# Planned arrival of eight heads' loads, filling of PE's gaps, and ten products of zeros, in the head of a fused attention and feed-forward kernel

## The chip, the cores and the metric

The kernel runs on one core of one Trainium2 chip. The metric is the device time of one execution in microseconds. The median of three runs of the kernel before is 440.37 us (439.73 to 440.39).

In what follows PE is the engine for matrix products, DVE the vector engine, ACT the scalar engine, POOL the engine whose queue issues the loads, SP the engine whose queue issues the stores and the transposing transfers. SBUF is the working memory, PSUM the memory into which PE writes, in eight banks.

## The reference

Attention with a squared ReLU in place of the softmax, then a gated feed-forward network over the tokens. All is given as float32.

```python
batch, n_heads, seq, head_dim = (8, 12, 448, 64)        # q, k, v
n_tokens, d_model, d_ff = (3584, 768, 1536)             # w_gate, w_val: 768x1536, w_out: 1536x768

scores = scale * np.matmul(q, k.transpose(0, 1, 3, 2))
attn = np.maximum(scores, 0.0) ** 2 / S
attn_out = np.matmul(attn, v)
x = np.ascontiguousarray(attn_out.transpose(0, 2, 1, 3)).reshape(B * S, H * D)

rms = np.sqrt(np.mean(x * x, axis=-1, keepdims=True) + 1e-06)
xn = x / rms * rms_g
g = xn @ w_gate
silu = g * (1.0 / (1.0 + np.exp(-g)))
val = xn @ w_val
return (silu * val @ w_out).astype(np.float32)
```

## The kernel before

**Tiling.** A batch is 448 tokens. Its twelve heads are worked on as six pairs (`j` from 0 to 5), since two heads of 64 fill the 128 partitions; two pairs (`j`, `j + 1`) form one group of value products. Scores are made transposed: keys on the partitions, queries along the row. The 448 keys are three blocks of 128 and a rest of 64; the rests of two pairs share one tile (`rest`). Batch 0 is done in two halves of 224 queries (`HS`, `scores_half`), so that the feed-forward part can begin on the first half; later batches are done whole.

**Stages of batch 0.** For each pair `transposes(b, j)` turns k and q on PE into a bank of PSUM: 14 small products read k from `wo_sb` (the space of the output weights serves k of batch 0, line 420) and 8 read q from `qb` (line 428). Then a copy moves the turned pair from PSUM to `qkT` (line 438 on DVE, or on ACT; the planner chooses). `scores_half` makes score products (line 502) and `rest` the rest (line 520) into double banks `psS`; `evict_rect` takes them out with a ReLU, on ACT (line 468) or DVE (line 466), and squares them on DVE (line 471). `attend` makes the value products (line 606), after which come the eviction to `xT` (lines 652 and 654), squares for the norm, their sums on PE (line 921), ln and exp on ACT (lines 729 and 733) and six scalings on DVE (line 738). The first gate and value products of the feed-forward part (line 873) read these. All that comes before them is called the head here.

**What sets the order.** No order is written out by hand. `Planner` keeps a model of each engine's free time. An `Op` has a cost for each engine that may do it, its dependences, and a rank; `Planner.run` always starts what can start earliest, and the order in which it starts the work is the order in which instructions are issued. So a figure in the model changes no duration on the chip, but can change the order of instructions on an engine, the engine of a copy or of a ReLU, and the bank that is used. In the model a load lands when `arrives(kb, rate)` says: all loads share one stream (`dma_free`), which moves `kb` kilobytes at `rate` kilobytes per microsecond.

**Loads.** All go through POOL's queue, in the order of the calls at the end: q and k of batch 0 in four parts (heads 0 and 1, 2 and 3, 4 to 7, 8 to 11), v in two parts, the gate and value weights in four quarters each, then batch 1 and the output weights. `load` plans the parts of q and k whose last head is 2 or 8 (that is heads 0 and 1, and heads 4 to 7) with 300 kilobytes per microsecond, the other parts with 340.

**Products of zeros.** `ones_bf` and `busy_bf` (ones and zeros) feed products of 128x224 whose result nobody reads. The planner calls `fill(t0, t1, late)` before each piece of PE work: `t0` is when PE becomes free in the model, `t1` when the next work starts. In the stretch called early (5.5 to 20 us of the model) it fills gaps from 0.15 us on, and as if they were 0.1 us longer, 0.5 us where the next work is a transpose (`late`); a product counts as 0.1 us there and the fill stops 0.15 us short of the lengthened end. Before 5.5 us a product counts as 0.19. The zeros go into one of the single banks `psP`, if one is free.

The order of the head that the planner writes for PE, in short: 22 products of zeros while the first loads are under way, pairs 0 and 1 transposed one after the other with zeros between, scores of these pairs with zeros between, pairs 2 and 3 transposed, three more score blocks, seven zeros, one score block, pairs 4 and 5 transposed, scores, seven zeros, the first value products.

## Time and profile before

| | |
|---|---|
| median of three runs | 440.37 us |
| the profiled execution | 441.04 us |
| its span, from the first to the last instruction | 439.3 us |
| PE busy | 432.9 us |
| ACT busy | 263.7 us |
| DVE busy | 256.2 us |
| granted clock of PE over the span | 1.000 |
| first gate product (line 873) starts | 27.52 us |
| a product of zeros in the first four microseconds | 0.185 us (22 weight loads in 4.07 us) |

A row of the timeline gives start, duration, engine, line, operation, output and input, and how often it comes in a row; a bracket at the end says how long the engine had been idle before it and what ended this. PE's instructions are pipelined, so a row of products lasts longer than the time after which the next row starts. Times within the head are from the start of the span.

### The profile page before, as it was taken

How to read it: one execution, taken by the hardware profiler on the slowest of the kernel's cores; microseconds unless marked ns; L12 is line 12 of the kernel's file. 1: busy time of each engine (PE TensorE's matmuls, PEld its weight loads, DVE VectorE, ACT ScalarE, POOL GpSimd, SP SyncE). 2: the span in 40 equal slices, each digit the busy share in tenths (PEclk: the TensorE clock that was granted, in tenths of full speed). 3: DMA queues.
4: the chain of work that ended last, by engine and by line, in shares of the span. 5: the costliest groups of instructions: out<-in, count | busy, mean ns of one | idle time of the engine just before them, and what ended most of it. 6: DMA issues, size and time to landing. Idle time of an engine off the chain costs nothing.

```text
span 439.3 us, 17167 instructions
## 1 busy us (share of the span) xinstructions
PE 432.9 (99%) x7861; PEld 351.4 (80%) x7861; DVE 256.2 (58%) x462; ACT 263.7 (60%) x390; POOL 47.1 (11%) x67
## 2 busy tenths in 40 slices
PE   8999999999999999999999999999999999999996
PEld 6668877677778677789988997689988997788865
DVE  2987588647955675486756556666755356432210
ACT  3783497539946765686758665586657656342222
POOL 8522400012012001200300012001000000000000
PEclk9999999999999999999999999999999999999999
DMA  8999995699669957896792899079001300020013
GB/s 98 193 204 202 201 206 77 111 194 117 75 79 172 163 81 92 108 155 114 102 120 66 131 151 123 8 137 171 4 3 37 106 7 3 1 85 27 3 37 109
DMA packets 82680, 44.75 MB, mean 102 GB/s; under 512 B 41904, under 2 KB 79152, under 8 KB 82608
## 3 DMA queue, kind: packets, MB, share of 16 engines
q0 software_dynamic: 43232, 24.38, 41.2%
q1 hardware_dynamic: 38992, 18.94, 22.0%
q8 instruction: 61, 1.00, 0.9%
q10 hardware_dynamic: 384, 0.34, 0.3%
q14 instruction: 11, 0.09, 0.1%
HBM read 48.76 MB, written 11.01 MB: 136 GB/s over the span
## 4 chain that ended last, share of the span: by engine, by line
PE 96%; DMA 1%; DVE 1%; issue 1%; POOL 0%; ACT 0%; POOLq 0%
PE psP L873 77%; PE psS L606 8%; PE psS L484 6%; PE psP L1152 1%; PE psS L520 1%; PE psP L428 1%; PE psS L502 1%; DMA wo_sb<-in_k_dram 1%; PE psP L420 0%; POOL qb L300 0%; PE psP L921 0%; DVE hT L958 0%; POOL wo_sb L284 0%; ACT xn L657 0%; DVE x L711 0%
## 5 line engine op out<-in xcount | busy, mean ns | idle before, releaser
L873 PE MATMUL psP<-xn,wg_sb 64*64 64x448 bf16 (+1 forms) x2304 | 235.0, 338 | 0.2 <-ACT sil L944 0.2
L873 PE MATMUL psP<-xn,wv_sb 64*64 64x448 bf16 (+1 forms) x2304 | 217.7, 338 | 0.1
L468 ACT ACTIVATE r<-psS 128x896 bf16<-128x896 f32 (+1 forms) x162 | 144.0, 925 | 55.7 <-PE psS L484 28.3
L873 PEld LDWEIGHTS <-wg_sb 64*64 64x64 bf16 (+1 forms) x2304 | 132.0, 105 | 17.8 <-issue 3.3
L873 PEld LDWEIGHTS <-wv_sb 64*64 64x64 bf16 (+1 forms) x2304 | 132.0, 105 | 16.1 <-issue 3.0
L873 PE MATMUL psP<-wo_sb,hT 64*128 64x384 bf16 (+2 forms) x1562 | 139.6, 321 | 0.0
L471 DVE TENSOR_TENSOR r<-r 128x896 bf16<-128x896 bf16 (+1 forms) x165 | 98.9, 617 | 60.3 <-ACT r L468 59.4
L873 PEld LDWEIGHTS <-hT 64*128 64x128 bf16 (+1 forms) x1562 | 100.1, 97 | 23.4 <-issue 3.2
L958 DVE TENSOR_TENSOR hT<-sil,psP 128x448 bf16<-128x448 bf16 (+1 forms) x108 | 61.1, 566 | 57.8 <-PE psP L873 44.1
L944 ACT ACTIVATE sil<-psP 128x448 bf16<-128x448 f32 (+1 forms) x108 | 54.9, 509 | 59.9 <-PE psP L873 55.1
L1018 ACT COPY ost<-psP 128x384 f32<-128x384 f32 (+1 forms) x55 | 25.9, 475 | 43.3 <-PE psP L873 42.8
L484 PE MATMUL psS<-qkT 64*64 64x448 bf16 (+1 forms) x420 | 48.1, 351 | 0.0
L606 PE MATMUL psS<-r,vb 64*64 64x448 bf16 (+1 forms) x716 | 44.2, 335 | 0.8 <-issue 0.6
L738 DVE SCALAR_TENSOR_TENSOR xn<-xT,g_sb,rstd 128x448 bf16<-128x448 bf16 (+1 forms) x54 | 30.2, 629 | 22.2 <-ACT rstd L733 22.1
L300 POOL DMA_DIRECT2D vb<-in_v_dram x20 | 14.3, 737 | 199.7 <-PE psP L873 132.7
L606 PEld LDWEIGHTS <-vb 64*64 64x64 bf16 x756 | 25.9, 106 | 9.5 <-issue 3.0
L654 ACT ACTIVATE xT<-psS 128x896 bf16<-128x896 f32 (+1 forms) x25 | 21.4, 857 | 10.2 <-PE psS L606 10.1
L484 PEld LDWEIGHTS <-qkT 64*64 64x64 bf16 (+1 forms) x420 | 22.2, 103 | 5.0 <-issue 0.7
L391 ACT ACT_TABLE_LOAD x16 | 20.5, 1283 | 1.0 <-PEq L1227 0.7
L669 DVE TENSOR_TENSOR x<-xT 128x896 f32<-128x896 bf16 x14 | 15.2, 1087 | 3.6 <-ACT xT L654 3.6
L671 DVE TENSOR_TENSOR acc<-acc,x 128x896 f32<-128x896 f32 x14 | 15.3, 1092 | 0.5
L300 POOL DMA_DIRECT2D qb<-in_q_dram x12 | 10.2, 854 | 42.5 <-DVE acc L671 14.0
(60 smaller groups left out, 158.3 us busy)
## 6 DMA issues: line engine op xcount, KB each, us to landing
vb<-in_v_dram POOLq DMA_DIRECT2D x12, 384.0 KB, 6.6
qb<-in_q_dram POOLq DMA_DIRECT2D x6, 672.0 KB, 8.3
out_dram<-ost SPq DMA_DIRECT2D x7, 336.0 KB, 3.0
wg_sb<-in_moe_w_gate_dram POOLq DMA_DIRECT2D x4, 576.0 KB, 15.5
wv_sb<-in_moe_w_val_dram POOLq DMA_DIRECT2D x4, 576.0 KB, 17.5
wo_sb<-in_moe_w_out_dram POOLq DMA_DIRECT2D x2, 1152.0 KB, 14.4
kb<-in_k_dram POOLq DMA_DIRECT2D x6, 384.0 KB, 8.9
out_dram<-ost SPq DMA_DIRECT2D x8, 288.0 KB, 2.8
```

The lines of the kernel that those rows point to most:

```text
L300: dma = nc.gpsimd.dma_start(out=stage(nm, b)[prt, h0:h1, : (u1 - u0) * D], in_=src.rearrange("h (p u) d -> p h (u d)", p=n)[:, :, u0 * D : ...
L391: nc.scalar.add_instruction(mybir.InstLoadActFuncSet(name=name, act_func_set_id=n, ins=[], outs=[]))
L468: nc.scalar.activation(out=op.view, in_=src, func=ACT.Relu)
L471: nc.vector.tensor_tensor(out=rl.view, in0=rl.view, in1=rl.view, op=ALU.mult)
L484: nc.tensor.matmul(out=ps[m0:m1, hh, :S], lhsT=qkT[b][prt, j, 0, c * P + m0 : c * P + m1], rhs=qkT[b][prt, j, 1, :], start=True, stop=True,)
L606: mm = nc.tensor.matmul(out=ps[hh * D : (hh + 1) * D, jj, :w], lhsT=vb[prt, 2 * (j + jj) + hh, u * D : (u + 1) * D], rhs=r[prt, hh, :], st ...
L654: nc.scalar.mul(out=to, in_=src, mul=inv_attn)
L738: nc.vector.scalar_tensor_tensor(out=xns[b][:, kt, lo : lo + w], in0=xTs[b][:, kt, lo : lo + w], scalar=g_sb[:, kt : kt + 1], in1=rstd[:, ...
L873: mm = nc.tensor.matmul(out=self.ps[m0:m1, : self.w], lhsT=self.lhsT(i)[prt, m0:m1], rhs=self.rhs(i)[prt], start=(half == 0 and i == 0), s ...
L944: nc.scalar.activation(out=s[:, :w], in_=g.ps[:, :w], func=ACT.Silu)
L958: nc.vector.tensor_tensor(out=hT[:, fb, o : o + w], in0=sil[b, fb, lo][1][:, :w], in1=g.ps[:, :w], op=ALU.mult,)
L1018: nc.scalar.copy(out=to, in_=g.ps[:, :w])
```

## The change

Three edits. `load` plans heads 4 to 7 of q and k of batch 0 with 340 instead of 300 kilobytes per microsecond; since all loads share one stream, every later load lands earlier in the model too. `fill` no longer lengthens gaps; in the early stretch it fills gaps from 0.2 us on, and stops 0.1 us short of their end. And `transposes` puts five products of zeros into its own bank ahead of pairs 2 and 4 of batch 0; the planned cost of these two, 0.52 us, stays.

```diff
             if e == "PE" and self.fill is not None:
-
-                self.fill(self.free["PE"], t, 0.4 if op != "step" and op.form == "t" else 0.0)
+                self.fill(self.free["PE"], t)
...
-            ops = [pool_dma(0.7, D * U * D * 4 * (h1 - h0) / 1e3, 300.0 if h1 in (2, 8) else 340.0, runs_of_seven, deps)]
+            ops = [pool_dma(0.7, D * U * D * 4 * (h1 - h0) / 1e3, 300.0 if h1 == 2 else 340.0, runs_of_seven, deps)]
...
-            ops.append(pool_dma(0.72, kb, (300.0 if h1 in (2, 8) else 340.0) if b == 0 else 400.0, whole, deps))
+            ops.append(pool_dma(0.72, kb, (300.0 if h1 == 2 else 340.0) if b == 0 else 400.0, whole, deps))
...
+    def busy(tile):
+        nc.tensor.matmul(out=tile[:, :HS], lhsT=ones_bf[:], rhs=busy_bf[:, :HS], start=True, stop=True)
+
     def transposes(b, j):
...
             op.flat = flat
+            if b == 0 and j in (2, 4):
+
+                for _ in range(5):
+                    busy(op.ps.tile)
             for u in range(U if b == 0 else 0):
...
-    def fill(t0, t1, late):
+    def fill(t0, t1):
 
         early = 5.5 < t0 < 20.0
-        if not fill_on[0] or t1 - t0 < (0.15 if early else 0.3):
+        if not fill_on[0] or t1 - t0 < (0.2 if early else 0.3):
             return
-        if early:
-            t1 += 0.1 + late
...
-        while t0 + (0.19 if t0 < 5.5 else 0.1) <= t1 - 0.15:
+        while t0 + (0.19 if t0 < 5.5 else 0.1) <= t1 - (0.1 if early else 0.15):
             t0 += 0.19 if t0 < 5.5 else 0.1
-            nc.tensor.matmul(out=s.tile[:, :HS], lhsT=ones_bf[:], rhs=busy_bf[:, :HS], start=True, stop=True)
+            busy(s.tile)
```

In the program that the planner then writes, POOL's instructions are those of before, in the same order. PE has 71 products of zeros instead of 81. Pair 2's copy is on ACT instead of DVE. The transposes of pairs 4 and 5 stand ahead of the score block that stood before them. Of the score tiles of pairs 2 and 3, the last wide ReLU goes from ACT to DVE and the narrow one of the rest from DVE to ACT. Behind the last attention blocks of the head the order of PE is the same in both.

## Prediction

> **What bounds the kernel now.** First the page's table of engines, then the table of busy time by stretch, which says where each engine is full.

> ```profile
> PE 432.9 (99%) x7861; PEld 351.4 (80%) x7861; DVE 256.2 (58%) x462; ACT 263.7 (60%) x390; POOL 47.1 (11%) x67
> ```

> ```profile
> 10.00:15.00 5.00, 5.00 (x100) 3.50 (x96) 4.36 (x9) 3.38 (x6) 3.19 (x4) 1.00 1.32 174
> 15.00:20.00 5.00, 4.81 (x98) 2.99 (x92) 4.58 (x10) 3.89 (x7) 3.38 (x5) 1.00 1.38 203
> 20.00:25.00 5.00, 4.78 (x90) 2.87 (x87) 4.98 (x11) 4.83 (x8) 1.00 (x2) 1.00 1.30 201
> 28.00:35.00 7.00, 7.00 (x137) 5.60 (x135) 5.64 (x14) 5.25 (x10) 1.63 (x3) 1.00 1.32 204
> ```

> The columns are the stretch, its length, busy time of PE, weight loads, DVE, ACT and POOL, then clock and DMA. From 28 us PE has no gap: a saved microsecond there must be PE work, and the change touches none. Everything it does lies before the first gate product of the feed-forward part (27.52 us). In that head PE looks full too, but part of its work is products of zeros; the engine that is full of real work from 15 to 25 us is DVE (4.58 and 4.98 of 5 us). So the question is when DVE's chain ends, not how many zeros are dropped.

> The timeline of the head gives the rest (start, duration, instruction, in brackets the idle time before it and what ended it):

> ```profile
> 6.22 1.13 PE L1152 MATMUL psP<-busy_bf,ones_bf 128*128 128x224 bf16 x10
> ...
> 7.58 0.41 PE L420 MATMUL psP<-ident,wo_sb 64*64 64x64 bf16 x14 [0.23 <-DMA wo_sb<-in_k_dram]
> ...
> 11.60 0.41 PE L420 MATMUL psP<-ident,wo_sb 64*64 64x64 bf16 x14
> ...
> 12.36 1.28 DVE L438 COPY qkT<-psP 128x896 bf16<-128x896 bf16 x2 [0.61 <-PE psP L428]
> ...
> 13.62 0.84 PE L1152 MATMUL psP<-busy_bf,ones_bf 128*128 128x224 bf16 x7
> ...
> 14.69 0.41 PE L420 MATMUL psP<-ident,wo_sb 64*64 64x64 bf16 x14
> ...
> 16.25 0.21 PE L428 MATMUL psP<-ident,qb 112*64 112x112 bf16 x1 [0.19 <-issue]
> ...
> 16.50 0.62 DVE L438 COPY qkT<-psP 128x896 bf16<-128x896 bf16 x1 [0.42 <-PE psP L428]
> ...
> 17.88 0.58 PE L606 MATMUL psS<-r,vb 64*64 64x224 bf16 x16
> 18.11 0.62 DVE L466 TENSOR_SCALAR r<-psS 128x448 bf16<-128x448 f32 x1
> ...
> 20.01 1.09 DVE L466 TENSOR_SCALAR r<-psS 128x896 bf16<-128x896 f32 x1
> ```

> The reader is to see that DVE waits for PE twice (0.61 and 0.42 us) and then runs without a hole from 16.50 to 24.98 us. Last, the landings of the two late loads of k, by issue:

> ```profile
> wo_sb<-in_k_dram POOLq DMA_DIRECT2D x1, 224.0 KB, 6.6
> ...
> wo_sb<-in_k_dram POOLq DMA_DIRECT2D x1, 224.0 KB, 7.7
> ```

> Issued at 4.96 and 6.26 us, they land at 11.56 and 13.96 us.

> **The change, part by part.** *Loads.* The figures are the planner's alone. POOL's list in the built program is the same, instruction for instruction, so no transfer moves; cost 0. What moves is the order that the planner writes for PE, ACT and DVE.

> *Zeros.* The built program has 71 products of zeros instead of 81. Steady ones start 0.0975 us apart (ten from 6.22 us), so 0.98 us of PE goes. Where each piece went from:
> - 10 to 6 ahead of pair 1 (pairs of heads are 0 to 5): PE idles 0.4 us longer, but heads 2 and 3 of k land at 7.52 (issue 3.32 plus 4.2), so 7.58 stays. If they landed early, up to 0.4 us would be gained there, and pair 1's copy with it.
> - 3 to 2, 5 to 4, 6 to 5 (before 9.1, 10.7, 11.6): the work behind them waits for a DVE copy (ends 8.97), an ACT eviction (ends 10.45) and the landing at 11.56. These hide the saving; 0 each.
> - 7 to 5 ahead of pair 4, and 7 to 6 ahead of the first value products: below.

> *Pair 2's copy goes from DVE to ACT.* ACT sits idle from 11.69 to 13.31. No row shows this copy on ACT; it lies between 0.62 (DVE's copy of the same tile) and 0.92 us (ACT's 128x896 eviction). I take 0.91, nearest in engine and size. It starts after pair 2's transposes (12.55) and ends at 13.2 to 13.5. Behind it wait ACT's next eviction (13.31 before, at most 0.2 later; its square on DVE has 0.26 us to spare) and the five zeros into the same bank, which have until 13.96. Price 0 to 0.1, I take 0.

> *Pairs 4 and 5 ahead of the score block that stood before them.* Before: seven zeros from 13.62, a score block at 14.39 that waits for an eviction, transposes at 14.69. Now: three score blocks to 13.62 as before, then five zeros (seven took 0.77, so 0.55) to 14.17; k has landed at 13.96; transposes at 14.17. From the first transpose of pair 2 to the copy of pair 3 it took 11.60 to 13.02, 1.42, so DVE's copy of pair 5 starts at 15.59 instead of 16.50: 0.91 earlier. Of this 0.39 comes from the hole marked "issue" at 16.25, in which PE waited for nothing shown: without it the copy would have begun at 14.69 + 1.42 = 16.11. The hole may reappear at another instruction, so this part is worth 0 to 0.39.

> *What DVE then has to do.* Its list from that copy to the wide ReLU at 20.01 was: copy, two squares, the narrow ReLU (18.11), two squares, xn's square: 3.51 us. The new list has the same, but a wide ReLU in place of the narrow one, which ACT gets. From rows: a wide one occupies DVE 1.00 (20.01 to 21.01), the narrow one 0.53 (18.11 to 18.64). So 3.51 + 0.47 = 3.98; 15.59 + 3.98 = 19.57 against 20.01: 0.44 earlier, 0.05 if the hole stays (0.44 less its 0.39).

> *First value products.* They wait for ACT's eviction of their bank: ACT works 0.8 apart on evictions, its next score block ends on PE near 15.9, so the eviction (0.92) ends at 16.9, v's second load (about 7.5 plus 9.1, 16.6) is in, and they start near 17.0, 0.9 earlier than 17.88. But what follows waits for squares from DVE, which come only 0.05 to 0.44 earlier. This is where most of the 0.9 goes: into idle PE or other waits. From 20 us on the lists of DVE are the same, and the first gate product follows through ln, exp and six scalings, unchanged: 27.1 to 27.5.

> *After it.* PE's order differs nowhere behind the head's last attention blocks. An earlier start could meet the weights: the last quarter of w_val lands at 42.33 (18.93 plus 23.4) and is first used at 43.98, spare 1.65, the smallest of the eight; 0.44 passes.

> **Sum.** -0.05 to -0.44 from DVE's chain, 0 to +0.1 for the copy; I take -0.2, near the middle, since one trace doesn't tell whether the hole stays. Profiled span 439.3, so 439.1; the profiled execution took 441.04, 1.7 us more than its span, and the median of the runs is 440.37, 0.67 below it. Carried to the median: 440.2.

> [...] In the rows, the first 22 zeros took 4.07 us, 0.185 each, the later ones 0.0975: PE starts at half rate and was fast from about 5.5 us. All later rows of the head are fast; the granted clock's column says 1.00 throughout and doesn't show this start. [...] No row of this trace shows a second slow spell.

> **Rivals.** *Slower: PE drops to half rate once more.* [...] In the kernel before, 5.5 to 9.7 us had 16 zeros, and stayed fast; now 11, and about 0.8 us idle instead of 0.4. For it: the drop did exist at the start. Against: PE still works three quarters of that stretch. Price: a spell as long as the first (4.2 us, 1.29 to 5.5) loses half, 2.1, less the waits that it fills (0.8 + 0.2 + 0.2): about 0.9 to 1.2, so 441.4.

> *Faster: the zeros were the bound.* The chain of waits over the first 35 us gives them the largest share:

> ```profile
> by line: PE psP L1152 16.5%; PE psS L606 16.1%; PE psP L873 15.1%; PE psS L502 13.5%; DMA wo_sb<-in_k_dram 12.0%; PE psP L428 5.1%; PE psP L420 5.0%; POOL qb L300 4.1%; issue 3.3%; PE psS L520 3.1%; POOL wo_sb L284 1.6%; ACT xn L657 1.6%; P
> ```

> If PE's list alone set the head, ten fewer give 0.98 and the value products' 0.9 would carry through: 439.4. Against: zeros stand where something else is waited for, and DVE is full.

> *It does nothing beyond the plan.* Transfers are the same; if the moved work meets the same DVE chain with the hole in place, 440.3. This ends with my forecast.

> **How the numbers follow.** Runs of this kernel spread from 439.73 to 440.39, so 0.2% (0.88 us) is about what can be told from no change. Forecast 0.50, the third rival 0.17, half rate 0.20, zeros as the bound 0.13. The forecast's own range is 439.6 to 440.7 (the runs' spread about it). Down to 439.4 it takes in the faster rival, up to 441.4 the middle of the slower one. A gain over 0.88 needs nearly all of the faster rival, so faster 0.11; slower 0.21; same 0.68.

> **What would show it.** Right: transposes of pair 4 near 14.15, pair 2's copy on ACT at 12.6, first value products near 17.0, DVE's wide ReLUs at 16.8 and 19.7, first gate product at 27.1 to 27.5, span 438.9 to 439.3. Wrong: zeros or score products in the head 0.185 apart (half rate); pair 4 well after 14.3 (a late load); DVE with holes between 16 and 25 us and a first gate product before 26.8 (zeros were the bound); or a new wait after 28 us.

## The result and the profile after

The changed kernel took 439.64 us, the median of 22 executions (438.77 to 440.38); the kernel before on the same chip took 440.35 us, also of 22 (439.48 to 441.47). The ratio is 0.9984, 95% interval 0.9976 to 0.9991: 0.7 us faster, by the interval 0.4 to 1.1. That is within the 0.2% named as hard to tell from no change, but more than three times the forecast's 0.2 us. On a second chip the same kernel stood at 440.01 us against 440.25, ratio 0.9995, interval 0.9987 to 1.0004, which is not clear of 1. A ratio, here and below, is estimated from all executions against those of the kernel before on the same chip; it is not the quotient of the two medians and can lie a little beside it. The profiled execution took 439.62 us, with a span of 437.8 us; the span of before's was 439.3.

First the page's table of engines and the busy time by stretch of the changed kernel, with the columns that were explained for the kernel before:

```profile
PE 431.1 (98%) x7851; PEld 350.3 (80%) x7851; DVE 256.0 (58%) x461; ACT 264.0 (60%) x391; POOL 47.1 (11%) x67
```

```profile
10.00:15.00 5.00, 4.33 (x96) 3.04 (x94) 3.82 (x8) 3.75 (x6) 3.03 (x4) 1.00 1.35 185
15.00:20.00 5.00, 5.00 (x98) 3.14 (x94) 4.97 (x10) 4.07 (x7) 3.54 (x5) 1.00 1.36 202
20.00:25.00 5.00, 4.75 (x86) 2.81 (x85) 4.84 (x10) 4.83 (x8) 1.39 (x2) 1.00 1.32 203
28.00:35.00 7.00, 7.00 (x141) 5.50 (x140) 5.26 (x14) 4.98 (x10) 1.31 (x2) 1.00 1.31 203
```

From 10 to 15 us PE now stands idle for 0.67 us. From 15 to 20 DVE is full (4.97 of 5 us, 4.58 before). The timeline of the head shows where each piece went:

```profile
7.41 0.41 PE L426 MATMUL psP<-ident,wo_sb 64*64 64x64 bf16 x14 [0.61 <-DMA wo_sb<-in_k_dram]
...
11.88 0.41 PE L426 MATMUL psP<-ident,wo_sb 64*64 64x64 bf16 x14 [0.67 <-DMA wo_sb<-in_k_dram]
...
12.64 0.91 ACT L446 COPY qkT<-psP 128x896 bf16<-128x896 bf16 x1 [1.20 <-PE psP L434]
...
13.90 0.65 PE L411 MATMUL psP<-busy_bf,ones_bf 128*128 128x224 bf16 x5
14.48 0.41 PE L426 MATMUL psP<-ident,wo_sb 64*64 64x64 bf16 x14
...
15.24 1.28 DVE L444 COPY qkT<-psP 128x896 bf16<-128x896 bf16 x2
...
16.97 1.08 DVE L472 TENSOR_SCALAR r<-psS 128x896 bf16<-128x896 f32 x1
17.16 0.58 PE L612 MATMUL psS<-r,vb 64*64 64x224 bf16 x16
...
19.88 1.08 DVE L472 TENSOR_SCALAR r<-psS 128x896 bf16<-128x896 f32 x1
```

Pair 2's transposes begin at 11.88, later than before (11.60): PE waited 0.67 us for k. All that follows stands closer together, and the first gate product comes at 27.24 instead of 27.52 us.

That is 0.28 us, and the spans differ by 1.4 (439.26 less 437.84 is 1.42). Laying the same products of both traces side by side, the changed kernel is 0.38 us ahead everywhere from 31 to 146 us, 1.2 us ahead from 147 us, and 1.43 us ahead from about 165 us to the end. At 147 us the timeline of the kernel before has a hole in the middle of sixteen value products:

```profile
146.24 0.38 PE L606 MATMUL psS<-r,vb 64*64 64x448 bf16 x3
147.18 0.94 PE L606 MATMUL psS<-r,vb 64*64 64x448 bf16 x13 [0.56 <-issue]
147.78 0.54 PE L520 MATMUL psS<-qkT 64*64 64x448 bf16 x4
```

The changed kernel has none there:

```profile
145.86 0.95 PE L612 MATMUL psS<-r,vb 64*64 64x448 bf16 x16
146.62 0.38 PE L526 MATMUL psS<-qkT 64*64 64x448 bf16 x4
```

From the first value product to the rest it is 1.54 us before and 0.76 after: 0.78 us, in a place that no edit touches. The bracket says that PE waited for nothing that the profile shows; v for these products had landed some 10 us earlier.

### The profile page after: what moved, and what is told of

The parts are those of the page before. It is cut to its first block, busy times and chain, and to the rows that moved or that the text cites. A ratio compares the mean times of both kernels' runs of the same rounds, so it can differ in the third digit from the quotient of the medians.

```text
span 437.8 us, 17149 instructions
## 1 busy us (share of the span) xinstructions
PE 431.1 (98%) x7851; PEld 350.3 (80%) x7851; DVE 256.0 (58%) x461; ACT 264.0 (60%) x391; POOL 47.1 (11%) x67
## 4 chain that ended last, share of the span: by engine, by line
PE 95%; DMA 2%; DVE 1%; POOL 1%; issue 0%; ACT 0%; POOLq 0%
PE psP L879 77%; PE psS L612 8%; PE psS L490 6%; DMA wo_sb<-in_k_dram 2%; PE psS L526 1%; PE psP L434 1%; PE psS L508 1%; PE psP L411 1%; POOL qb L299 0%; PE psP L426 0%; PE psP L927 0%; POOL wo_sb L283 0%; DVE hT L964 0%; ACT xn L663 0%; DVE x L717 0%
## 5 line engine op out<-in xcount | busy, mean ns | idle before, releaser
L879 PEld LDWEIGHTS <-hT 64*128 64x128 bf16 (+1 forms) x1562 | 100.1, 97 | 23.4 <-issue 3.2
L490 PE MATMUL psS<-qkT 64*64 64x448 bf16 (+1 forms) x420 | 47.2, 351 | 0.0
L299 POOL DMA_DIRECT2D vb<-in_v_dram x20 | 14.3, 736 | 194.9 <-PE psP L879 188.1
L675 DVE TENSOR_TENSOR x<-xT 128x896 f32<-128x896 bf16 x14 | 15.2, 1087 | 3.6 <-ACT xT L660 3.6
L677 DVE TENSOR_TENSOR acc<-acc,x 128x896 f32<-128x896 f32 x14 | 15.3, 1092 | 0.5
## 6 DMA issues: line engine op xcount, KB each, us to landing
wg_sb<-in_moe_w_gate_dram POOLq DMA_DIRECT2D x4, 576.0 KB, 15.4
```

What stands on the lines that cost most here:

```text
L299: dma = nc.gpsimd.dma_start(out=stage(nm, b)[prt, h0:h1, : (u1 - u0) * D], in_=src.rearrange("h (p u) d -> p h (u d)", p=n)[:, :, u0 * D : ...
L490: nc.tensor.matmul(out=ps[m0:m1, hh, :S], lhsT=qkT[b][prt, j, 0, c * P + m0 : c * P + m1], rhs=qkT[b][prt, j, 1, :], start=True, stop=True,)
L879: mm = nc.tensor.matmul(out=self.ps[m0:m1, : self.w], lhsT=self.lhsT(i)[prt, m0:m1], rhs=self.rhs(i)[prt], start=(half == 0 and i == 0), s ...
```

## The experiments

Two things had to be told apart: what the edits do in the head, and whether the hole belongs to the change. A third question came from the slower rival: do the ten products keep PE's clock up?

**Both kernels again.** The kernel before, unchanged, one execution:

> The kernel before, unchanged, profiled once more, to see which of its holes marked 'issue' on PE come back (0.19 us at 16.25, 0.56 us at 147.18). If holes belong to the execution: both are absent or elsewhere, and the first gate product starts at 27.2 to 27.5. If they belong to the program's place in memory: both come back within 0.3 us of the same instruction. Span 438.0 to 440.5 either way.

It took 441.21 us, span 439.4. The hole in the head at 16.25 is gone; the one at 147 is there again, at the same product:

```profile
147.04 0.94 PE L606 MATMUL psS<-r,vb 64*64 64x448 bf16 x13 [0.34 <-issue]
```

The changed kernel, unchanged:

> The changed kernel, unchanged, profiled and timed once more. Theory 1 (DVE's chain in the head plus chance holes later): first gate product at 27.2 to 27.5, the same instruction at 60 us within 0.2 us of the first profile, time 0.2 to 0.7 us below the kernel before. Rival (the program's layout makes the holes): no hole over 0.3 us behind 30 us in this one either, time 0.7 us below.

It took 440.01 us (11 executions), as told above; span of the profiled one 437.5, first gate product at 26.90, no hole. So the hole at 16.25 was chance, and the one at 147 had come in both profiles of the kernel before and in neither of the changed one.

**One part at a time.** Only the loads' figures (340 instead of 300, as in the diff), on the kernel before:

> The kernel before with the new load plan alone (340 for heads 4 to 7): pairs 4 and 5 are transposed ahead of the score block, pair 2's copy is on ACT, fill as before, no five products. Theory 1 (the moved transposes feed DVE's chain earlier): the whole gain of the head, first gate product 0.2 to 0.4 us earlier than in the kernel before, time 439.9 to 440.2 against 440.4. Rival (fewer zeros bring it): first gate product as before, no gain.

439.75 us (12), ratio 0.9994, interval 0.9969 to 1.002. This edit alone gives the changed order of work. The first gate product comes at 27.12, yet the profiled span is 439.4, since a hole has opened in the same block of value products, ten products further on:

```profile
145.75 0.92 PE L606 MATMUL psS<-r,vb 64*64 64x448 bf16 x13
148.05 0.38 PE L606 MATMUL psS<-r,vb 64*64 64x448 bf16 x3 [1.39 <-issue]
```

Only the new filling, on the kernel before:

```diff
-        if not fill_on[0] or t1 - t0 < (0.15 if early else 0.3):
+        if not fill_on[0] or t1 - t0 < (0.2 if early else 0.3):
...
-            t1 += 0.1 + late
+            pass
...
-        while t0 + (0.19 if t0 < 5.5 else 0.1) <= t1 - 0.15:
+        while t0 + (0.19 if t0 < 5.5 else 0.1) <= t1 - (0.1 if early else 0.15):
```

> The kernel before with the new fill rule alone: 68 products of zeros instead of 81, order of the real work as before. Theory 1: zeros stand where something else is waited for, so the first gate product stays within 0.1 us and the time within 0.2 us of the kernel before. Rival (zeros were the bound): 13 fewer at 0.0975 us, up to 1.2 us earlier.

439.91 us (11), ratio 1.0003, interval 0.9984 to 1.0021; first gate product 26.64. Against the second profile of the kernel before (27.48) that is 0.84 us earlier, but 0.65 of it stands already at pair 2, which began at 11.30 instead of 11.95; behind pair 2 it is 0.19. Only the ten products, on the kernel before:

```diff
+            if b == 0 and j in (2, 4):
+                for _ in range(5):
+                    nc.tensor.matmul(out=op.ps.tile[:, :HS], lhsT=ones_bf[:], rhs=busy_bf[:, :HS], start=True, stop=True)
```

> The kernel before with the two times five products of zeros alone, fill and load plan as before (91 products of zeros). They stand behind zeros that already reach to the transposes, so each five (0.49 us) pushes the transposes back. Theory 1: from pair 1's first transpose to pair 2's takes 4.0 plus 0.5 = 4.5 us, from pair 2's first transpose to the first gate product 15.5 plus up to 0.5 us, time 440.7 to 441.4. Rival (the five products help by themselves, by keeping PE at full rate): no slower than the kernel before.

440.80 us (11), ratio 1.0017, interval 1.0002 to 1.0032: slower, with the first gate product at 27.87. With the old filling in place the ten are extra work on the path: pair 2 begins 4.49 us behind pair 1, where the kernel before took 4.02 and 4.01 in its two profiles.

**Zeros taken out of the changed kernel.** Without the ten products (`j in ()` in place of `j in (2, 4)`):

> The changed kernel without the two times five products of zeros (61 left); new load plan and new fill rule stay. Theory 1: pair 4's transposes wait for k's landing instead of the zeros, at most 0.2 us earlier; from pair 2's first transpose to the first gate product 15.2 to 15.4 us, as in the changed kernel (15.36); time within 0.3 us of it. Rival (the products are needed to keep PE at full rate): products in the head 0.185 us apart in some stretch, first gate product 0.9 us or more later.

442.31 us (10), ratio 1.0054, interval 1.0034 to 1.0073: the changed kernel less its ten products is slower than the kernel before. The busy time by stretch of this kernel shows why; the granted clock is the third number from the right:

```profile
14.00:15.00 1.00, 0.74 (x22) 0.68 (x22) 1.00 (x3) 1.00 (x2) 0.91 (x2) 0.70 1.46 191
15.00:16.00 1.00, 1.00 (x28) 0.79 (x24) 0.95 (x2) 0.79 (x2) 0.86 (x2) 0.50 1.45 195
...
20.00:21.00 1.00, 1.00 (x20) 0.59 (x20) 0.00 (x0) 0.27 (x1) 0.00 (x0) 0.50 1.25 192
21.00:22.00 1.00, 1.00 (x11) 0.32 (x7) 0.69 (x2) 1.00 (x3) 0.00 (x0) 0.89 1.33 204
```

And its timeline, where twelve score products last 1.23 us to the start of the zeros, and six zeros 1.24 to the next row (18.72); in the changed kernel it is 0.68 and 0.69:

```profile
11.91 0.41 PE L426 MATMUL psP<-ident,wo_sb 64*64 64x64 bf16 x14 [1.25 <-DMA wo_sb<-in_k_dram]
...
16.25 1.30 PE L508 MATMUL psS<-qkT 64*128 64x224 bf16 x12
17.48 1.30 PE L411 MATMUL psP<-busy_bf,ones_bf 128*128 128x224 bf16 x6
...
29.66 0.36 PE L879 MATMUL psP<-xn,wg_sb 64*128 64x224 bf16 x2
```

The clock is halved from 14.40 us (0.70 in a stretch of 1 us is 0.60 us at half rate) to 21.22: 6.82 us. The first gate product comes at 29.66, 17.75 behind pair 2's first transpose, where the changed kernel needs 15.36: 2.4 us more. This profile is of the slowest of the ten executions (445.01 us): besides the clock it has three holes, and the part behind its first gate product is 2.9 us longer than in the changed kernel.

Without any zeros that the planner writes between 5.5 and 20 us, the ten included (31 of 71 are left):

```diff
-            if b == 0 and j in (2, 4):
+            if b == 0 and j in ():
...
-        if not fill_on[0] or t1 - t0 < (0.2 if early else 0.3):
+        if early or not fill_on[0] or t1 - t0 < (0.2 if early else 0.3):
```

> The changed kernel without any product of zeros between 5.5 and 20 us of the plan: the 22 at the start and those behind 20 us stay, 31 in all. Theory 1 (zeros only fill waits, DVE's chain sets the end): PE's idle time in the head grows by some 2.5 us, the first gate product stays within 0.2 us of the changed kernel's place behind pair 2's transposes (15.36 us). Rival half rate: score products 0.15 us apart instead of 0.075 in some stretch of the head, first gate product 0.9 to 1.7 us later, time 440.5 to 441.5. Rival zeros as the bound: first gate product 0.5 us or more earlier.

442.20 us (8), ratio 1.0048, interval 1.0031 to 1.0066. The clock falls earlier, at 9.76 us, and stays down to 26.82:

```profile
9.00:10.00 1.00, 0.59 (x8) 0.29 (x5) 0.58 (x2) 1.00 (x2) 0.61 (x1) 0.88 0.99 118
10.00:11.00 1.00, 0.40 (x4) 0.13 (x3) 1.00 (x3) 1.00 (x3) 0.09 (x1) 0.50 1.19 151
...
26.00:27.00 1.00, 1.00 (x15) 0.45 (x15) 0.63 (x2) 1.00 (x2) 0.00 (x0) 0.59 1.31 203
```

The clock is not all of it here. Three of the eight executions have a mean granted clock of 0.999 or 1.000 and still took 442.04 to 443.04 us, longer than three with 0.983 to 0.988 (441.03 to 441.55). What these three lost stays open.

**Which five.** The ten products were then split, on the changed kernel. The five ahead of pair 2 alone (`j in (2,)`):

> The changed kernel with the five products ahead of the second pair kept and those ahead of the fourth left out (66 products of zeros). Theory A: TensorE's clock falls where it has stood or only transposed too long, and the longest such stretch is the wait for k ahead of the second pair (0.17 to 1.25 us in the runs so far) with the transposes right behind it; then the five there are what is needed, the clock stays at 1.00 through 14 to 21 us, 14 transposes take 0.26 to 0.32 us, the first gate product comes about 15.4 us after the second pair's first transpose, and the time is 439.6 to 440.1 us. Theory B: the five ahead of the fourth pair, where three pairs are transposed close together and PE waits for k again, are the ones that are needed; then the clock falls to 0.5 to 0.6 from 14 us on as without the ten, and the time is 442 to 443 us.

440.09 us (12), ratio 1.0003, interval 0.9979 to 1.0027. The five ahead of pair 4 alone (`j in (4,)`):

> The changed kernel with the five products ahead of the fourth pair kept and those ahead of the second left out (66 products of zeros). Theory A: the clock falls to 0.5 to 0.6 in the stretch 11 to 17 us, as without the ten, and the time is 442 to 443 us. Theory B: the clock stays at 1.00 and the time is 439.6 to 440.1 us. If both this kernel and the one with the five ahead of the second pair stay at 1.00, either five are enough; if both fall, all ten are needed.

441.81 us (12), ratio 1.0028, interval 1.0002 to 1.0055. Neither profile shows the clock down, but the mean granted clock of each execution does: 5 of 12 executions with the five at pair 4 have 0.988 to 0.991, and 2 of 12 with the five at pair 2 have 0.992. Neither five alone is enough, and the third outcome named there, that all ten are needed, is nearest. That the place ahead of pair 2 matters more, as theory A has it, is likely from 2 against 5 of 12, not shown. The profile with the five at pair 4 has two other losses instead:

```profile
14.84 0.41 PE L426 MATMUL psP<-ident,wo_sb 64*64 64x64 bf16 x14 [0.72 <-DMA wo_sb<-in_k_dram]
...
148.69 0.38 PE L526 MATMUL psS<-qkT 64*64 64x448 bf16 x2 [1.19 <-issue]
```

The first is the late part of k: when it lands late, the new order of pairs 4 and 5 waits for it. The profile with the five at pair 2 met an early one and shows what the five at pair 4 cost then: pair 4 starts at 13.74, 2.32 behind pair 2 instead of 2.60, and the first gate product at 26.51, the earliest of all.

**Two of three parts.** Loads' figures and ten products, with the old filling (91 products of zeros):

> The kernel before with the loads planned by the 340s and the ten products, and the old filling of gaps (91 products of zeros). If the gain of the change is the order of the work alone, this has the order and time of the changed kernel: first gate product 15.3 to 15.4 us behind the second pair's first transpose, 439.6 to 440.1 us. If zeros ahead of the pairs cost what the old filling and the ten put there, it is 0.3 to 0.5 us later, near the kernel before or above it (the ten alone on the kernel before gave 440.80 us).

439.92 us (12), ratio 0.9995, interval 0.9979 to 1.001; first gate product 27.08, 15.65 behind pair 2's first transpose. New filling and ten products, with the old figures (78 products of zeros):

> The changed kernel with the loads planned by the 300s as before (78 products of zeros): the new filling and the ten products on the old order of the work. If the new order is what gains, this has the time of the kernel before, 440.2 to 440.5 us; if the shorter filling gains and the ten products keep the clock up, 439.6 to 440.1 us and the first gate product 15.3 to 15.5 us behind the second pair's first transpose.

440.12 us (12), ratio 1.0, interval 0.9984 to 1.0016; first gate product 27.25, 15.93 behind. From pair 2's first transpose to the first gate product the two kernels with the new order and all ten products need 15.36 (changed) and 15.65, the two with the old order 15.93 and 16.11 (ten products only). Without the ten it is 15.53 before, 15.30 with the figures alone and 15.34 with the filling alone. So in these profiles, one or two of each kernel, either part shortens the head by 0.2 us, and it is the new order that makes room for the ten. But in the new order pair 4 stands one score block earlier in PE's list and can meet k still on its way: where it waited for k, by 0.72 us with the five at pair 4 and by 0.64 in the kernel shifted by 20 (below), the same stretch took 16.15 and 16.07, longer than in the kernel before. The medians of the last two kernels, 0.2 us apart with intervals of 0.16%, don't tell them apart.

**The hole.** If the place of an instruction in PE's list alone opened it, the changed kernel with 20 PE instructions more at its start would have its value products at the place of the kernel before. Four of the first 22 zeros are cut into fourteen small ones:

```diff
+            zeros[0] += 1
+            if zeros[0] <= 4:
+                for _ in range(4 if zeros[0] <= 2 else 3):
+                    nc.tensor.matmul(out=s.tile[:32, :D], lhsT=ones_bf[:, :32], rhs=busy_bf[:, :D], start=True, stop=True)
+            else:
+                busy(s.tile)
```

> The changed kernel with four of the 22 products of zeros at the start cut into 14 of 64 columns, same streamed columns. It adds 20 instructions on PE, so every later instruction has the place in the list that it has in the kernel before. Theory 1 (holes marked 'issue' belong to the execution): no difference, span 437.4 to 438.6, time within 0.3 us of the changed kernel. Rival (the place in the list decides): the hole of the kernel before at 147 us is back, three value products into their block, 0.3 to 0.9 us, and the time is 0.3 to 0.7 us above the changed kernel's.

440.09 us (12), ratio 1.0004, interval 0.9985 to 1.0023; no hole at 147 in its profile. The place alone does not open it. But it does say where a hole can be: counted from the start of PE's list, the holes near 147 us stand ahead of the same product, the 2524th, in every kernel that has one, whatever number of zeros comes before (the last section sets the starts of instruction packets beside them).

**All profiles, taken apart.** The work behind the first gate product is the same in all fourteen, 7446 products. Rest is the span less the first gate product's start; holes are the idle times of PE that the timeline marks "issue" behind it.

| kernel | zeros | first gate product | rest | holes (us, at) |
|---|---|---|---|---|
| before, again | 81 | 27.52, 27.48 | 411.8, 411.9 | 0.56 at 147; 0.34 at 147 |
| changed, again | 71 | 27.24, 26.90 | 410.6, 410.6 | none |
| figures only | 71 | 27.12 | 412.3 | 1.39 at 148 |
| filling only | 68 | 26.64 | 411.4 | 0.26 at 110 |
| ten products only | 91 | 27.87 | 410.7 | none |
| figures and ten | 91 | 27.08 | 410.9 | none marked |
| filling and ten | 78 | 27.25 | 411.3 | none marked |
| five at pair 2 | 66 | 26.51 | 410.7 | none |
| five at pair 4 | 66 | 27.60 | 412.3 | 1.19 at 149 |
| shifted by 20 | as changed, 4 cut | 27.30 | 411.0 | none |
| no ten products | 61 | 29.66 | 413.5 | 0.68, 1.16, 0.34 at 101, 152, 280 |
| no zeros 5.5 to 20 us | 31 | 30.69 | 411.3 | none marked |

A single product's row lasts 0.35 us there, while the next product starts long before its end (sixteen start within 0.76 us in the changed kernel), so a short stop leaves no idle time that could be marked. It shows in a row that lasts too long. With filling and ten products, the sixteen value products at 147 us take 0.52 us longer than in the changed kernel:

```profile
145.95 1.47 PE L612 MATMUL psS<-r,vb 64*64 64x448 bf16 x16
```

Against the usual time between the same two products, figures and ten lost 0.4 us in this way at 109.34, and the kernel without zeros 0.4 at 102.99.

A time is the sum of two things that vary on their own: the head, which the edits move, and a rest of 410.6 to 411.4 us without or with a small hole and 411.8 to 413.5 with others. The rest differs by more than the head does in the kernels that keep their clock (26.51 to 27.87), and it is no property of one kernel: of fourteen profiles six have marked holes, both of the kernel before and four with other edits, and three more a stop of 0.4 us or more that has no mark.

The mean granted clock of every execution gives the other half, since a stretch at half rate lowers it (6.82 us of 443.2 at half is 0.992):

| kernel | executions at 0.992 or below |
|---|---|
| before (the three sets with a clock on record) | 0 of 93 |
| changed (both chips) | 0 of 33 |
| ten products only; figures and ten; filling and ten | 0 of 11; 0 of 12; 0 of 12 |
| filling only; shifted by 20 | 1 of 11; 1 of 12 |
| figures only; five at pair 2 | 2 of 12; 2 of 12 |
| five at pair 4 | 5 of 12 |
| no zeros 5.5 to 20 us | 5 of 8 |
| no ten products | 8 of 10 |

A single spell of 3.41 us, the step between the clock's changes in two traces (last section), would be 0.996. One execution of the kernel before has that (443.67 us), one more with the five at pair 2 (443.17) and one more without the ten (441.38). So the kernel before is not quite free of it: 1 of 93.

No version is shown to be faster than the changed kernel. Figures only and figures and ten (ratios 0.9994 and 0.9995) can't be told from it. The two with the earliest first gate product (five at pair 2, filling only) have the clock down in some executions, and their ratios to the kernel before, both 1.0003, are no better than the changed kernel's 0.9984 and 0.9995.

## Why the prediction was right, and where it was not

**The bound: DVE's sum right, the last stretch of the head and the part behind it not.** With its start moved to where pair 2 really began (0.28 us later than in the kernel before), the working follows the trace closely as far as DVE's last wide ReLU. Pair 4's transposes were put at 14.17; 14.45 with the shift, and they came at 14.48. DVE's copy of pair 5: 15.59 plus 0.28 is 15.87, and the second of the two copies from 15.24 begins half of 1.28 later, at 15.88. The wide ReLU: 19.57 plus 0.28 is 19.85, and it came at 19.88. The first value products: 17.0 plus 0.28, and they came at 17.16. From pair 2's first transpose to the wide ReLU the changed kernel needs 8.00 us, the kernel before 8.41 with the hole at 16.25 and 8.03 without it (second profile): 0.41 and 0.03 less, where the sum has 0.44 and 0.05.

Behind that ReLU the prediction had everything "unchanged". There the first gate product gains another 0.14 us. DVE waits for ACT in this stretch, less long in the changed kernel. First the kernel before:

```profile
20.36 1.36 ACT L468 ACTIVATE x<-psS 128x896 bf16<-128x896 f32 x2
...
25.44 0.62 DVE L652 TENSOR_SCALAR xT<-psS 128x448 bf16<-128x448 f32 x1 [0.46 <-ACT xn L657]
```

Then the changed kernel:

```profile
20.07 1.38 ACT L474 ACTIVATE x<-psS 128x896 bf16<-128x896 f32 x2
...
25.16 0.62 DVE L658 TENSOR_SCALAR xT<-psS 128x448 bf16<-128x448 f32 x1 [0.32 <-ACT xn L663]
```

ACT evicts there without a gap (18.41 to 24.44 us in the changed kernel). Its first eviction to `x` comes 0.29 us earlier, the wide ReLU only 0.13, and the first gate product follows the eviction by 7.16 and 7.17 us. So DVE's chain accounts for the head up to 20 us; that ACT's list sets the rest is read from these rows, and no run tested it. The profile's chain of waits can't decide it: it names PE, zeros included, and one eviction of ACT, but the zeros cover what PE would have waited for.

But "From 28 us PE has no gap" was read from a single row, 28 to 35 us. The same trace held the hole at 147.18. With what PE lost around it, this is the larger part of the difference between the profiled spans: 1.05 of 1.43 us. The span of 438.9 to 439.3 was missed (437.8) by this; with 1.05 us more it would have been 438.9. The sum was made against one execution's span, which carried a loss that other executions of the same kernel need not have.

**Loads: 0, right as to their issue.** Their landings are another matter: from one profile to the next pair 2 waits for k by nothing to 1.25 us (by 0.84 with the figures only, which have the old filling), and pair 4 by nothing to 0.72. The prediction named pair 4 well after 14.3 as the sign of a late load. It came at 14.48, and the late load was the one ahead of it, that of pair 2.

**Zeros ahead of pair 2: "these hide the saving; 0 each" held in the first profile, by the landing.** The landing at 11.56 and the last of six zeros fell together in the one trace shown. In both profiles of the kernel before pair 2 began 4.02 and 4.01 us behind pair 1 with no wait for k: PE's list set it. With the shorter filling PE is free earlier, and the landing decides. In the first profile of the changed kernel k came late, and pair 2 began 4.47 behind pair 1, so nothing was gained. Where it came early it was 3.97 (changed, again), 3.94 (five at pair 2) or 3.73 (shifted by 20). So this term is worth from nothing to 0.3 us, and the prediction, with one landing in hand, had no range for it.

**Pair 2's copy on ACT: right.** 0.91 us was taken and 0.91 measured, at 12.64 for a forecast 12.6; nothing behind it was late.

**The hole at 16.25: rightly left open.** It came in one of two profiles of the kernel before and in no other. Without it the kernel before needs 15.53 us from pair 2 to the first gate product (as in its second profile), the changed one 15.36 and 15.37: 0.17 us from the edits together. That it lies near the 0.2 taken is in part luck: 0.2 was the middle between a hole that stays (0.05) and one that goes (0.44). Without the hole on either side the sum has 0.05, and the 0.17 is 0.03 from DVE's chain and 0.14 from behind it, for which the sum has no term.

**The rivals.** *Half rate* was real (the clock fell at 14.4 us without the ten products and at 9.8 without the zeros), but not in this kernel: the ten products are what keeps it away (0 of 33 executions with them, 8 of 10 without). Its price was put at 0.9 to 1.2 us for a spell of 4.2; the spell in the trace without them lasted 6.82 and delayed the first gate product by 2.4. *Zeros as the bound* falls for the whole head: with zeros and products taken out, pair 2 and pair 4 wait for k (1.25 and 0.26 us without the ten), and the clock goes. In small it holds: the filling alone leaves the order of the work as it was and still brings the first gate product 0.19 us nearer to pair 2 (15.34 against 15.53, one profile each). For the same reason *nothing beyond the plan* falls too.

**The size.** In the head the gain is about the forecast's, and on the second chip it is all of it (440.25 less 440.01, not clear of noise). What is left of the 0.7 us on the first chip is not in any term of the sum. Of 115 executions of the kernel before 37 lie above 440.5 us, of 33 of the changed kernel none; fewer holes would look like this. That the change makes them rarer is argued, not shown: the changed kernel shifted by 20 instructions has 4 of 12 above 440.5 (one of them by its clock), and what came ahead of every marked hole, an instruction packet that starts late (last section), is late in one execution and not in another for a reason that stays open.

## What to carry to other kernels

Before making a sum against one profiled execution, look along the whole span for holes that no edit explains, and compare a second profile: the part that your edits don't touch can differ by more than they bring (here a rest of 410.6 to 413.5 us, for a head shorter by 0.2). A hole that no wait explains may be a late packet of instructions (here every marked hole ended 2.3 to 2.6 us behind a packet's start): see whether it comes back at the same place of the engine's list, and when that packet started. Products of zeros are insurance for the clock rather than filler: what they cost is read from where real work waits behind them, what they are worth only from how often the clock falls without them, so count executions, not one trace (here 8 of 10 at 0.992 or below without the ten, 0 of 33 with them). And a saving that is "hidden by a landing" is worth whatever the landing's spread allows (here nothing to 0.3 us).

## What the runs showed of the hardware

**In two traces the clock's changes lay whole multiples of 3.41 us apart, and the first came at no fixed time.** The traces hold the moments at which the granted clock changes. Without the ten products it opens at 4.15 us (the zeros at the start go from 0.187 to 0.097 us apart there), falls at 14.39 and opens again at 21.22: 10.24 and 6.83 us, three and two times 3.41. Without the zeros of 5.5 to 20 us it opens at 6.34, falls at 9.75 and opens at 26.82: 3.41 and 17.07 us, one and five times. In all fourteen profiles PE's first product starts at 1.29 or 1.30 us, yet the clock first opens anywhere from 3.97 to 6.97. In the first profiles it is 5.70 for the kernel before and 5.03 for the changed one. Whether this spread is why the clock falls in some executions of a program and not in others, no run here shows.

The fall at 14.39 did not follow a long stop of PE: in the 3.41 us before it PE stood idle 0.92 us at the start (10.99 to 11.91) and 0.26 near the end, with 44 transposes and 12 score products between. In the next 3.41 us, to 17.81, PE was busy for all of it, transposes for more than half (up to 16.25), and the clock stayed down. PE's busy time alone does not say whether the clock opens. At the start it opened after 2.68 us of zeros (1.29 to 3.97, figures and ten), but after 3.18 us of work between 19.99 and 23.41, nearly all score and value products, it did not (without the zeros). The rows give the zeros as 128*128, score and value products as 64*128 and 64*64; whether a product's size or kind counts, no run varied alone.

**Holes stand whole multiples of 256 PE instructions apart.** In the first profile of the kernel before the holes at 16.25 and 147.18 are 4609 PE instructions apart, weight loads counted, which is 18 times 256 and 1. All marked holes of the other profiles stand at that distance too, to one instruction: ahead of the 1629th, 1885th, 2524th and 4954th product, 11, 13, 18 and 37 times 256 instructions behind the one at 16.25. The page's queue table for the changed kernel has a line for instructions:

```profile
q8 instruction: 61, 1.00, 1.0%
```

The traces have the start of every such packet. Taking the first packet for the place of the hole at 16.25 and the following ones for the places 256 instructions further on each, every marked hole ends 2.3 to 2.6 us after the start of its packet:

| profile | packet starts | PE goes on | later by |
|---|---|---|---|
| before | 13.89; 144.80 | 16.25; 147.18 | 2.36; 2.38 |
| before, again | 144.49 | 147.04 | 2.55 |
| figures only | 145.58 | 148.05 | 2.47 |
| filling only | 107.64 | 109.98 | 2.34 |
| five at pair 4 | 146.15 | 148.69 | 2.54 |
| no ten products | 98.79; 149.17; 277.71 | 101.22; 151.65; 280.02 | 2.43; 2.48; 2.31 |

In all fourteen profiles no product at such a place starts less than about 2.2 us behind the start of its packet. In the changed kernel the packet for the 2524th product starts at 140.92, and the product comes 5.5 us later, without a stop. So PE goes on much the same time, 2.3 to 2.6 us, behind the start of a packet that is late, and from these rows the holes are read as its wait for the next 256 instructions; no run moved a packet by itself. Why the packet starts late in one execution and not in another, no run here shows. The marked holes measured 0.19 to 1.39 us.
